# A long convolution with a rational feed-forward: the rounds of the first convolution in another order, and the products u on GpSimd

## The chip, the cores and the metric

One core of a Trainium2 chip. Its engines work side by side, each on its own queue in order: TensorE (PE, matmuls, with its weight loads shown as PEld), VectorE (DVE), ScalarE (ACT), GpSimd (POOL) and SyncE (SP, which here issues DMAs). They meet by semaphores. The metric is the device time of one execution in microseconds; before the change it is 2475.74 us, the median of 3 runs (2475.0 to 2476.28).

## What is computed

The reference filters u = x * v with a long filter by FFT, multiplies the result by x, and sends every token through a gated rational function between two matrices:

```python
# attention part, x and v: (2, 12480, 128), pos_emb: (12480, 64), w1: (64, 64), w2: (64, 128)
h_filt = (np.maximum(pos_emb @ w1, 0.0) @ w2) * np.exp(-0.01 * pos)[:, None]
u = x * v
L = 2 * S
y = np.fft.irfft(np.fft.rfft(u, n=L, axis=1) * np.fft.rfft(h_filt, n=L, axis=0)[None, :, :], n=L, axis=1)[:, :S, :]
x = (x * y).reshape(24960, 128)
# mixture part, w_in: (128, 2048), w_out: (2048, 128), a: 4 numbers, b: 2
h = x @ w_in
P = a[0] + a[1] * h + a[2] * h * h + a[3] * h * h * h
Q = 1.0 + np.abs(b[0]) * np.abs(h) + np.abs(b[1]) * h * h
out = (P / (Q + 1e-06)) @ w_out
```

## The kernel before

The convolution over 12480 positions is a transform in two factors, each done by matmuls with a constant matrix and a multiplication with twiddle factors between. The 128 channels are cut into 32 groups of 4 (CG = 4, NG = 32); eight groups are a quarter of the channels, 32 (UQ). A quarter of u lies in one buffer (tiles `hu0` to `hu3`, printed `hu_` with a number); it is filled by eight products of x and v, each of 16 positions of the second factor (UC) and all 32 channels (`mult_quarter`, L234), and a MEMSET on GpSimd (L229) clears its padding.

The program has four stages. **The filter's network** (0 to about 85 us of the trace): a loop of transposes and two matmuls makes the filter's values `hf`; `hf_w` multiplies the position embedding by the decaying window, the lower half in one TENSOR_TENSOR (L470), the mirrored half in four TENSOR_SCALAR (L474), for 16 blocks. Between them generators hand out one piece each time: the weights of the mixture, cut into two parts of high and low precision (`to_f32`, lines 320 to 336 and 445, where GpSimd's L331 feeds DVE's L336), and the eight products of the first quarter of u, on GpSimd. **The rounds** (85 to 375 us): the convolution of batch 0 together with the filter's transform. **The second part** (375 to 2440 us): a loop over steps of the mixture, with the convolution of batch 1 in its slots until about 1320 us. **The end** stores the last tiles.

A round g works on up to four groups, in a pipeline. In the order in which the instructions are written:

- s1h(g), the filter's first transform: matmuls L146 with `hf` into a PSUM tile `cs`, then six operations of DVE (`s1h_out`, L552, L553, L557 to L560) that write `zh`.
- s2h(g-1), the filter's second: L564 from `zh`; ACT copies the spectrum to `hg` (L600) and sends it to memory for batch 1 (L601).
- s1(g-1), the first transform of u: matmuls L146 with `hu`, two twiddle products on DVE (L164, L165) and two sums on GpSimd (L170, L171) that write `zu`.
- s2(g-2), the second of u: L181 to L184 from `zu`; DVE multiplies by `hg` (L196, L197), GpSimd sums (L199, L200) into `yy`.
- s3p(g-3), the inverse: L571 from `yy`; ACT copies twice (L578), GpSimd adds and subtracts (L582, L583) into `ys`, which two groups share. Every second round ACT copies a part of ys to `y0` (L621), which the second part begins with, and sends the whole to memory (L622).
- one product of the next quarter of u, on DVE (`mult_u`), as long as there are any (24, in rounds 0 to 23), else a piece of the weights; then the loads for a later product.

So there are 35 rounds, g = 0 to 34. The PSUM tiles `cs` of all five matmul groups come from one pool of four buffers, ys from a pool of one buffer, the other tiles named from pools of two. No scheduler moves anything: each engine runs its instructions in the order written.

In the second part a step s holds two halves of a block. ACT's work of a step is q0, v0 (squares and linear terms of the first half, L868, L877), q1, v1 of the second, ln of the step before (L905), sq (L901) and exp of the step before (L908). DVE finishes v (L887) and makes the ratio (L913, L918, L922). The change touches ACT's order in the loop at the end of `second_part`.

Of the kernel before, what the change touches and what calls it, by code (L numbers as in the profile page):

```python
# [9 lines left out]
F32 = mybir.dt.float32  # L10
F32R = mybir.dt.float32r
I32 = mybir.dt.int32
AF = mybir.ActivationFunctionType
# [87 lines left out]
def build(ctx: ExitStack, tc, x, v, pos_emb, w1, w2, w_in, w_out, moe_a, moe_b,  # L101
# [145 lines left out]
    with ExitStack() as st:  # L247
# [219 lines left out]
        def hf_w(p0):  # L467
# [4 lines left out]
            for i in range(NPL):  # L472
                n2 = H2 - 1 - p0 - i
                nc.vector.tensor_scalar(out=pw[:, i, 1], in0=t[0:MF, 2 * NPL - 1 - i], scalar1=win[0:MF, n2:n2 + 1],  # L474
                                        scalar2=None, op0=ALU.mult)
# [112 lines left out]
        for g in range(NG + 3):  # L588
            a = g
            if a < NG:  # L590
                zh[a] = ctile(sp, "zh", 2, CG)
                t = cvs()
                s1_mm(t, hf[a // gq], a % gq * CG, CG, MF)
                s1h_out(t, zh[a])
            a = g - 1
            if 0 <= a < NG:
                hgs[a] = ctile(sp, "hg", 2, CG)
# [4 lines left out]
                zu[a] = ctile(sp, "zu", 2, CG)  # L602
                t = cvs()
                s1_mm(t, us[a // gq], a % gq * CG, CG)
                s1_out(sp, t, zu[a], CG)
            a = g - 2
            if 0 <= a < NG:
                yy[a] = ctile(sp, "yy", 2, CG)
                t = cvs()
                s2_mm(t, zu.pop(a), CG)  # L610
                s2_prod(sp, t, hgs.pop(a), yy[a], CG)
            a = g - 3
            if 0 <= a < NG:
                if a % 2 == 0:
                    ysd[a // 2] = ystile(sp)
                t = cvs()
                s3p_mm(t, yy.pop(a))
                s3p_out(t, ysd[a // 2], a % 2 * CG, (nc.gpsimd, nc.gpsimd if a < NG - 3 else nc.vector))
                if a % 2 == 1:
                    t = ysd.pop(a // 2)  # L620
                    nc.scalar.activation(out=y0[:, a // 2], in_=t[:, :, 0:NPT, :], func=AF.Identity)  # L621
                    nc.scalar.dma_start(out=y_d[0][:, a // 2], in_=t)  # L622
            if uw and gq * (uw[0][0] - 1) <= g:
                mult_u(nc.vector)
# [10 lines left out]
    def second_part(short):  # L635
# [365 lines left out]
        for s in range(ns + 3):  # L1001
# [5 lines left out]
            run(s, dve_v, 0)  # L1007
            run(s, act_q, 1)
            run(s - 1, act_ln)
# [3 lines left out]
            run(s, act_v, 1)  # L1013
            run(s, act_sq)
            run(s + 1, mm1, 1)
            run(s, dve_v, 1)
            run(s - 1, act_exp)
            run(s - 2, dve_g)
# [35 lines left out]
```

## Time and profile before

| | |
|---|---|
| device time, median of 3 runs | 2475.74 us (2475.0 to 2476.28) |
| the profiled execution | 2475.52 us, its span 2473.6 us |
| busy in the span | PE 86%, DVE 94%, ACT 85%, POOL 22% |
| granted TensorE clock, mean | 0.969 of full speed |
| the filter's network, 0 to 84.7 us | DVE busy 69.4 us, PE 59.0, ACT 53.3, POOL 28.2 |
| rounds 0 to 22, 84.7 to 268.3 us | DVE 181.1 us of 183.6, PE 173.8, POOL 138.8 |
| rounds 23 to 27, 268.3 to 326 us | DVE 54.6 us of 57.7, PE 43.9 |
| the other rounds, 326 to 374.9 us | PE 43.1 us of 48.9, DVE 37.0 |
| 400 to 1300 us | DVE 848.6 us of 900, ACT 820.8, PE 808.7 |
| 1400 to 2440 us | ACT 1039.0 us of 1040, DVE 1023.6 |

The shares are averages over stages with different limits, so a stage is read by its own windows. A row of the timeline gives the start, the duration, the engine and line, the operation with its output and input, and in brackets how long the engine stood idle ahead of it and whom it waited for. Durations on one engine overlap a little, since the next instruction starts before the one before it has written all; the distance of starts is what an operation costs.

### The profile page before, as it was taken

The numbers are of one execution on the slowest core, as the hardware profiler recorded it, in microseconds if no ns is written. First come the engines' busy times: TensorE is split into PE (matmuls) and PEld (weight loads), VectorE is DVE, ScalarE is ACT, GpSimd is POOL, SyncE is SP. The second block draws the span as 40 slices with busy tenths as digits, with TensorE's granted clock in tenths as the row PEclk, the third lists the DMA queues.
The fourth block names the chain that finished last, engine by engine and source line by source line (L and its number), as shares of the span: only waits on it lengthen the run. The fifth ranks groups of instructions, "written<-read, shape, count | busy, mean of one in ns | idle before, by whom it ended". The sixth has DMA issues, their size and how long they took to land.

```text
span 2473.6 us, 33923 instructions
## 1 busy us (share of the span) xinstructions
PE 2129.4 (86%) x13344; PEld 1799.1 (73%) x13344; DVE 2335.8 (94%) x1945; ACT 2098.8 (85%) x1919; POOL 534.7 (22%) x522
## 2 busy tenths in 40 slices
PE   6899886999899979998999889788888888888786
PEld 4677765877777868777787777667777777767665
DVE  8999976999999988998999999999999999999997
ACT  5322227999999978998999999999999999999996
POOL 3488663121522242226122100000000000000000
PEclk9999997999999989999999999999999999999999
DMA  7466328112521252214222111111111111111000
GB/s 145 101 144 145 93 92 157 39 50 55 109 59 45 69 91 57 59 46 85 58 65 59 35 39 43 43 30 32 39 30 36 40 32 40 43 32 41 26 13 11
DMA packets 357824, 150.25 MB, mean 61 GB/s; under 512 B 292518, under 2 KB 339752, under 8 KB 354776
## 3 DMA queue, kind: packets, MB, share of 16 engines
q1 hardware_dynamic: 350632, 124.24, 23.8%
q10 hardware_dynamic: 7024, 23.76, 3.0%
q8 instruction: 107, 1.75, 0.3%
q14 instruction: 61, 0.50, 0.1%
HBM read 99.78 MB, written 48.17 MB: 60 GB/s over the span
## 4 chain that ended last, share of the span: by engine, by line
ACT 35%; DVE 27%; PE 24%; issue 9%; POOL 2%; DMA 1%; SPq 0%; ACTq 0%; DVEq 0%; POOLq 0%
ACT r L908 9%; ACT r L905 9%; ACT q L868 7%; PE acc L936 7%; DVE v L922 7%; ACT v L877 6%; DVE r L918 4%; DVE q L913 4%; PE cv L205 3%; ACT q L901 2%; PE cv L206 2%; DVE ta L192 2%; DVE v L887 2%; PE cs L571 2%; PE cv L146 1%
## 5 line engine op out<-in xcount | busy, mean ns | idle before, releaser
L936 PE MATMUL acc<-wout,v 128*128 128x128 f32 (+2 forms) x6656 | 829.2, 283 | 59.8 <-DVE v L922 35.2
L936 PEld LDWEIGHTS acc<-wout,v 128*128 128x128 f32 (+2 forms) x6656 | 785.0, 192 | 111.8 <-DVE v L922 53.9
L877 ACT ACTIVATE v<-h,sc 128x980 f32<-128x980 f32 (+1 forms) x416 | 639.0, 1536 | 6.6 <-PE acc L936 6.6
L868 ACT ACTIVATE q<-h 128x980 f32<-128x980 f32 (+1 forms) x416 | 581.5, 1455 | 6.6 <-PE h L860 6.6
L887 DVE SCALAR_TENSOR_TENSOR v<-v,sc,h 128x980 f32<-128x980 f32 (+1 forms) x416 | 505.8, 1216 | 62.1 <-ACT v L877 60.5
L901 ACT ACTIVATE q<-q,sc 128x1960 f32<-128x1960 f32 (+1 forms) x208 | 494.9, 2380 | 0.0
L905 ACT ACTIVATE r<-q,sc 128x1960 f32<-128x1960 f32 (+1 forms) x208 | 494.1, 2375 | 0.3 <-DVE v L922 0.3
L908 ACT ACTIVATE r<-r 128x1960 f32<-128x1960 f32 (+1 forms) x208 | 475.8, 2288 | 0.0
L913 DVE SCALAR_TENSOR_TENSOR q<-q,sc,r 128x1960 f32<-128x1960 f32 (+1 forms) x208 | 467.7, 2249 | 4.8 <-ACT r L908 1.1
L922 DVE SCALAR_TENSOR_TENSOR v<-v,sc,r 128x1960 f32<-128x1960 f32 (+1 forms) x208 | 465.6, 2238 | 0.1
L858 PE MATMUL h<-ahi,win_l 128*128 128x490 f32 (+1 forms) x832 | 364.3, 438 | 102.5 <-DVE v L887 100.1
L918 DVE SCALAR_TENSOR_TENSOR r<-q,r 128x1960 f32<-128x1960 f32 (+1 forms) x208 | 451.2, 2169 | 0.1
L859 PE MATMUL h<-alo,win_h 128*128 128x490 f32 (+1 forms) x832 | 320.7, 385 | 0.0
L860 PE MATMUL h<-ahi,win_h 128*128 128x490 f32 (+1 forms) x832 | 318.1, 382 | 0.0
L858 PEld LDWEIGHTS h<-ahi,win_l 128*128 128x128 f32 x832 | 158.5, 191 | 161.6 <-DVE v L887 133.9
L199 POOL TENSOR_TENSOR yy<-ta 128x180 f32<-128x180 f32 x64 | 119.8, 1871 | 369.5 <-DVE ta L192 369.5
L860 PEld LDWEIGHTS h<-ahi,win_h 128*128 128x128 f32 x832 | 158.8, 191 | 26.4
L859 PEld LDWEIGHTS h<-alo,win_h 128*128 128x128 f32 x832 | 159.2, 191 | 15.8 <-DVE alo L829 0.4
L804 PE MATMUL cv<-yc,gt 90*98 90x128 f32 x1004 | 131.8, 279 | 35.2 <-DVE an L810 32.6
L804 PEld LDWEIGHTS cv<-yc,gt 90*98 90x98 f32 x1004 | 115.7, 166 | 55.3 <-DVE an L810 51.5
L209 ACT ACTIVATE ys<-cv 90x512 f32<-90x512 f32 x64 | 77.0, 1203 | 71.6 <-PE cv L206 71.6
L205 PE MATMUL cv<-idft,yy 128*90 128x256 f32 x256 | 79.9, 394 | 61.2 <-DVE ta L192 36.4
(109 smaller groups left out, 2395.6 us busy)
## 6 DMA issues: line engine op xcount, KB each, us to landing
yc<-y_d SPq DMA_DIRECT2D x23, 900.0 KB
gt<-in_g_dram SPq DMA_DIRECT2D x48, 344.5 KB
h_d<-hg ACTq DMA_DIRECT2D x32, 360.0 KB
y_d<-ys ACTq DMA_DIRECT2D x16, 720.0 KB
hg<-h_d SPq DMA_DIRECT2D x64, 180.0 KB
y_d<-ys SPq DMA_DIRECT2D x16, 720.0 KB
xq<-in_x_dram SPq DMA_DIRECT2D x32, 196.0 KB
vq<-in_v_dram SPq DMA_DIRECT2D x32, 196.0 KB
```

What stands on the lines that cost most here:

```text
L858: nc.tensor.matmul(out=t[:, k, 0:w], lhsT=wl, rhs=hi[:, 0:w], start=True, stop=False)
L859: nc.tensor.matmul(out=t[:, k, 0:w], lhsT=wh, rhs=lo[:, 0:w], start=False, stop=False)
L868: nc.scalar.activation(out=halves(st_q[s], i, width(s)), in_=st_h[s, i], func=AF.Abs, **({} if short else {"scale": col("b0")}))
L877: nc.scalar.activation(out=v, in_=st_h[s, i], func=AF.Square, bias=col("s"))
L887: stt(out=v, in0=v, scalar=col("k"), in1=h, op0=ALU.add, op1=ALU.mult)
L901: nc.scalar.activation(out=whole(st_q, s), in_=whole(st_q, s), func=AF.Square, bias=col("dl"))
L905: nc.scalar.activation(out=whole(st_r, s), in_=whole(st_q, s), func=AF.Ln, **({"bias": col("ka")} if short else {}))
L908: nc.scalar.activation(out=whole(st_r, s), in_=whole(st_r, s), func=AF.Exp, scale=-1.0)
L913: nc.vector.scalar_tensor_tensor(out=q, in0=q, scalar=col("ka") if short else 0.0, in1=whole(st_r, s), op0=ALU.add, op1=ALU.mult)
L918: nc.vector.scalar_tensor_tensor(out=r, in0=whole(st_q, s), scalar=2.0, in1=r, op0=ALU.subtract, op1=ALU.mult)
L922: nc.vector.scalar_tensor_tensor(out=v, in0=v, scalar=col("p0" if short else "a0"), in1=whole(st_r, s), op0=ALU.add, op1=ALU.mult)
L936: nc.tensor.matmul(out=acc[j][0:k, q // 128, :], lhsT=g[:, i, q:q + k], rhs=wout[:, f, :], start=(f == 0 and q == 0), stop=(f == NF - 1), ...
```

## The change

Four edits. `hf_w` makes the mirrored half of the window product with one TENSOR_TENSOR of 82x256, by negative strides. The rounds are written as s1h(g), s1(g), s2(g-1), s3p(g-2), s2h(g), which makes 34 of them; the last ys tile lies in a buffer of the pool of hu, and of the last groups' sums on ys, one addition and two subtractions are DVE's (before, three subtractions). The products u in the rounds are GpSimd's. In the second part's step, ln stands ahead of q1, and exp ahead of sq. Lines behind L472 move by one, in the second part by nine.

```diff
--- before.py
+++ after.py
@@ -469,10 +469,11 @@
             pw = pos_t[p0] = sp.tile([MF, NPL, 2, FO], F32, tag="wb", name="pw", bufs=2)
             nc.vector.tensor_tensor(out=pw[:, :, 0], in0=t[0:MF, 0:NPL],
                                     in1=win[0:MF, H2 + p0:H2 + p0 + NPL].unsqueeze(2).to_broadcast([MF, NPL, FO]), op=ALU.mult)
-            for i in range(NPL):
-                n2 = H2 - 1 - p0 - i
-                nc.vector.tensor_scalar(out=pw[:, i, 1], in0=t[0:MF, 2 * NPL - 1 - i], scalar1=win[0:MF, n2:n2 + 1],
-                                        scalar2=None, op0=ALU.mult)
+
+            a, w = t[0:MF, 2 * NPL - 1], win[0:MF, H2 - 1 - p0:H2 - p0]
+            a = bass.AP(a.tensor, a.offset, [list(a.ap[0]), [-FO, NPL], [1, FO]])
+            w = bass.AP(w.tensor, w.offset, [list(w.ap[0]), [-1, NPL], [0, FO]])
+            nc.vector.tensor_tensor(out=pw[:, :, 1], in0=a, in1=w, op=ALU.mult)
 
         def hf_t(i):
             p0 = i * NP
@@ -585,43 +586,51 @@
         zh, zu, hgs, yy, ysd = {}, {}, {}, {}, {}
         gq = UQ // CG
 
-        for g in range(NG + 3):
+        def ys_tile(i):
+
+            if i < NG // 2 - 1:
+                return ystile(sp)
+            t = sp.tile([M, UQ, N2], F32, tag="hu", name="ysl", bufs=6)
+            return t.rearrange("p c t -> p (c t)")[0:K1, 0:2 * N2 * CY].rearrange("p (r t c) -> p r t c", r=2, t=N2)
+
+        for g in range(NG + 2):
             a = g
             if a < NG:
                 zh[a] = ctile(sp, "zh", 2, CG)
                 t = cvs()
                 s1_mm(t, hf[a // gq], a % gq * CG, CG, MF)
                 s1h_out(t, zh[a])
+                zu[a] = ctile(sp, "zu", 2, CG)
+                t = cvs()
+                s1_mm(t, us[a // gq], a % gq * CG, CG)
+                s1_out(sp, t, zu[a], CG)
             a = g - 1
             if 0 <= a < NG:
+                yy[a] = ctile(sp, "yy", 2, CG)
+                t = cvs()
+                s2_mm(t, zu.pop(a), CG)
+                s2_prod(sp, t, hgs.pop(a), yy[a], CG)
+            a = g - 2
+            if 0 <= a < NG:
+                if a % 2 == 0:
+                    ysd[a // 2] = ys_tile(a // 2)
+                t = cvs()
+                s3p_mm(t, yy.pop(a))
+                s3p_out(t, ysd[a // 2], a % 2 * CG, (nc.gpsimd if a < NG - 1 else nc.vector,
+                                                     nc.gpsimd if a < NG - 2 else nc.vector))
+                if a % 2 == 1:
+                    t = ysd.pop(a // 2)
+                    nc.scalar.activation(out=y0[:, a // 2], in_=t[:, :, 0:NPT, :], func=AF.Identity)
+                    nc.scalar.dma_start(out=y_d[0][:, a // 2], in_=t)
+            a = g
+            if a < NG:
                 hgs[a] = ctile(sp, "hg", 2, CG)
                 t = cvs()
                 s2h_mm(t, zh.pop(a))
                 nc.scalar.activation(out=hgs[a].rearrange("p r c k -> p r (c k)"), in_=spectrum(t, CG), func=AF.Identity)
                 nc.scalar.dma_start(out=h_d[:, a], in_=hgs[a])
-                zu[a] = ctile(sp, "zu", 2, CG)
-                t = cvs()
-                s1_mm(t, us[a // gq], a % gq * CG, CG)
-                s1_out(sp, t, zu[a], CG)
-            a = g - 2
-            if 0 <= a < NG:
-                yy[a] = ctile(sp, "yy", 2, CG)
-                t = cvs()
-                s2_mm(t, zu.pop(a), CG)
-                s2_prod(sp, t, hgs.pop(a), yy[a], CG)
-            a = g - 3
-            if 0 <= a < NG:
-                if a % 2 == 0:
-                    ysd[a // 2] = ystile(sp)
-                t = cvs()
-                s3p_mm(t, yy.pop(a))
-                s3p_out(t, ysd[a // 2], a % 2 * CG, (nc.gpsimd, nc.gpsimd if a < NG - 3 else nc.vector))
-                if a % 2 == 1:
-                    t = ysd.pop(a // 2)
-                    nc.scalar.activation(out=y0[:, a // 2], in_=t[:, :, 0:NPT, :], func=AF.Identity)
-                    nc.scalar.dma_start(out=y_d[0][:, a // 2], in_=t)
             if uw and gq * (uw[0][0] - 1) <= g:
-                mult_u(nc.vector)
+                mult_u(nc.gpsimd)
             else:
                 next(wg, None)
             load_u()
@@ -1005,16 +1014,16 @@
             run(s - 2, dve_e)
             slot(s, 0)
             run(s, dve_v, 0)
+            run(s - 1, act_ln)
             run(s, act_q, 1)
-            run(s - 1, act_ln)
+            run(s, act_v, 1)
             run(s - 3, mm2)
             run(s - 2, dve_n)
             slot(s, 1)
-            run(s, act_v, 1)
-            run(s, act_sq)
             run(s + 1, mm1, 1)
             run(s, dve_v, 1)
             run(s - 1, act_exp)
+            run(s, act_sq)
             run(s - 2, dve_g)
             slot(s, 2)
             if s >= 3 and steps[s - 3][1] == NC - 1:
```

PE, where group 16, the first of the third quarter, is transformed (groups 8 and 24 stand alike). In the names, hf1 and hf2 are the second and third quarter of the filter, hu1 and hu2 those of u; the other numbers only tell tiles apart. Before, round 16 with a part of round 17:

```order
L571 MATMUL cs_1919<-idfth_90,yy_1841 90x128 x8
L146 MATMUL cs_1940<-f1_66,hf2_93 128x180 x4
L564 MATMUL cs_1953<-zh_1875,dfth_89 128x360 x2
L146 MATMUL cs_1959<-f1_66,hu1_992 128x180 x4
L181 MATMUL cs_1971<-zu_1894,dft_68 128x360
L182 MATMUL cs_1971<-zu_1894,dft_68 128x360
L183 MATMUL cs_1971<-zu_1894,dft_68 128x360
L184 MATMUL cs_1971<-zu_1894,dft_68 128x360
L571 MATMUL cs_1982<-idfth_90,yy_1906 90x128 x8
L146 MATMUL cs_2007<-f1_66,hf2_93 128x180 x4
L564 MATMUL cs_2020<-zh_1939,dfth_89 128x360 x2
L146 MATMUL cs_2026<-f1_66,hu2_1473 128x180 x4
```

After, the end of round 15 and round 16:

```order
L572 MATMUL cs_1910<-idfth_90,yy_1834 90x128 x8
L565 MATMUL cs_1928<-zh_1873,dfth_89 128x360 x2
L146 MATMUL cs_1939<-f1_66,hf2_93 128x180 x4
L146 MATMUL cs_1952<-f1_66,hu2_1471 128x180 x4
L181 MATMUL cs_1964<-zu_1886,dft_68 128x360
L182 MATMUL cs_1964<-zu_1886,dft_68 128x360
L183 MATMUL cs_1964<-zu_1886,dft_68 128x360
L184 MATMUL cs_1964<-zu_1886,dft_68 128x360
L572 MATMUL cs_1976<-idfth_90,yy_1898 90x128 x8
```

Before, the first matmuls on hu2 stand a whole round behind the first on hf2; after, they stand right behind them, in the same round, and s2h (L565) stands last in the round instead of second.

GpSimd, the rounds of the same kind. Before, a round and the start of the next:

```order
L170 TENSOR_TENSOR zu<-ta,tb 128x360
L171 TENSOR_TENSOR zu<-ta,tb 128x360
L199 TENSOR_TENSOR yy<-pta,ptb 128x360
L200 TENSOR_TENSOR yy<-pta,ptb 128x360
L582 TENSOR_TENSOR ys<-qt 90x128x4
L583 TENSOR_TENSOR ys<-qt 90x2x64x4
L170 TENSOR_TENSOR zu<-ta,tb 128x360
```

After, round 7 with the last product of the second quarter at its end, and the start of round 8:

```order
L170 TENSOR_TENSOR zu_1360<-ta_1366,tb_1367 128x360
L171 TENSOR_TENSOR zu_1360<-ta_1366,tb_1367 128x360
L199 TENSOR_TENSOR yy_1372<-pta_1378,ptb_1379 128x360
L200 TENSOR_TENSOR yy_1372<-pta_1378,ptb_1379 128x360
L583 TENSOR_TENSOR ys_1320<-qt_1393,qt_1395 90x128x4
L584 TENSOR_TENSOR ys_1320<-qt_1393,qt_1395 90x2x64x4
L234 TENSOR_TENSOR hu1_962<-xq_1277,vq_1278 97x16x32
L170 TENSOR_TENSOR zu_1425<-ta_1431,tb_1432 128x360
L171 TENSOR_TENSOR zu_1425<-ta_1431,tb_1432 128x360
L199 TENSOR_TENSOR yy_1437<-pta_1443,ptb_1444 128x360
L200 TENSOR_TENSOR yy_1437<-pta_1443,ptb_1444 128x360
```

The last product into hu1 (L234) stands behind zu, yy and both sums of ys, and zu of round 8 stands behind it; before, no product stood on this engine here.

ACT in the loop of the second part, one step. Before, with L868 q, L877 v, L905 ln, L901 sq, L908 exp:

```order
L868 ACTIVATE q<-h 128x980
L877 ACTIVATE v<-h,sc 128x980
L868 ACTIVATE q<-h 128x980
L905 ACTIVATE r<-q,sc 128x1960
L877 ACTIVATE v<-h,sc 128x980
L901 ACTIVATE q<-q,sc 128x1960
L908 ACTIVATE r<-r 128x1960
```

After, with L877 q, L886 v, L914 ln, L910 sq, L917 exp:

```order
L877 ACTIVATE q<-h 128x980
L886 ACTIVATE v<-h,sc 128x980
L914 ACTIVATE r<-q,sc 128x1960
L877 ACTIVATE q<-h 128x980
L886 ACTIVATE v<-h,sc 128x980
L917 ACTIVATE r<-r 128x1960
L910 ACTIVATE q<-q,sc 128x1960
```

ln moved ahead of the second q, and exp ahead of sq; the other places are the same.

## Rows read from the trace of the kernel before

**Rows 1.** Windows: length; busy us of PE, PEld, DVE, ACT, POOL; granted clock; DMA.

```profile
120.00:152.00 32.00, 29.66 (x168) 23.96 (x168) 31.57 (x44) 7.93 (x14) 25.47 (x24) 1.00 0.61 143
333.80:341.60 7.80, 7.80 (x45) 6.43 (x44) 7.18 (x11) 2.12 (x4) 5.87 (x7) 1.00 0.38 109
290.00:300.00 10.00, 6.37 (x28) 6.05 (x29) 9.89 (x14) 1.57 (x4) 5.02 (x6) 0.66 0.41 116
```

**Rows 2.** Timeline of DVE, end of a product round: start us, us, operation.

```profile
177.26 1.10 DVE L234 TENSOR_TENSOR hu<-xq,vq 98x512 f32<-98x512 f32 x1
178.21 0.89 DVE L552 TENSOR_TENSOR tb<-cs,twh 128x720 f32<-128x720 f32 x1
```

**Rows 3.** Timeline of PE, late round without the product: inverse transform, next round's first.

```profile
338.36 1.91 PE L571 MATMUL cs<-idfth,yy 128*90 128x128 f32 x16
340.11 1.39 PE L146 MATMUL cs<-f,hf 82*128 82x180 f32 x8
```

**Rows 4.** Timeline of DVE and POOL in the same late round.

```profile
333.76 0.91 DVE L552 TENSOR_TENSOR tb<-cs,twh 128x720 f32<-128x720 f32 x1 [0.52 <-POOL zu L171]
337.15 0.54 DVE L560 TENSOR_TENSOR zh<-cs,tb 64x360 f32<-64x360 f32 x1
342.15 0.95 POOL L200 TENSOR_TENSOR yy<-pta,ptb 128x360 f32<-128x360 f32 x1
336.44 1.26 POOL L583 TENSOR_TENSOR ys<-qt 90x512 f32<-90x512 f32 x1
```

**Rows 5.** Timeline of PE: a short wait, and a long one later.

```profile
272.39 1.95 PE L571 MATMUL cs<-idfth,yy 128*90 128x128 f32 x16 [0.48 <-DVE zh L560]
293.63 3.69 PE L571 MATMUL cs<-idfth,yy 128*90 128x128 f32 x16 [5.38 <-DVE zh L560]
297.12 1.94 PE L146 MATMUL cs<-f,hf 82*128 82x180 f32 x8
```

**Rows 6.** Timeline of the first stage: POOL's product of u, DVE's window product twice.

```profile
17.26 1.28 POOL L234 TENSOR_TENSOR hu<-xq,vq 98x512 f32<-98x512 f32 x1 [3.48 <-DMA vq<-in_v_dram]
17.39 1.42 DVE L470 TENSOR_TENSOR pw<-pos,ta 82x256 f32<-82x256 f32 x1 [2.44 <-DMA pos<-in_pos_emb_dram]
54.27 0.42 DVE L470 TENSOR_TENSOR pw<-pos,ta 82x256 f32<-82x256 f32 x1
```

**Rows 7.** Timeline of DVE: L552 of rounds 23 and 25.

```profile
268.33 0.90 DVE L552 TENSOR_TENSOR tb<-cs,twh 128x720 f32<-128x720 f32 x1
289.57 0.90 DVE L552 TENSOR_TENSOR tb<-cs,twh 128x720 f32<-128x720 f32 x1
```

**Rows 8.** Timeline of the start: L552 of rounds 0 and 2, PE between.

```profile
84.68 0.90 DVE L552 TENSOR_TENSOR tb<-cs,twh 128x720 f32<-128x720 f32 x1
96.21 0.90 DVE L552 TENSOR_TENSOR tb<-cs,twh 128x720 f32<-128x720 f32 x1
87.61 2.74 PE L564 MATMUL cs<-zh,dfth 128*128 128x360 f32 x4 [3.78 <-issue]
```

**Rows 9.** Timeline of the end: L552 of rounds 28 and 31, last ys.

```profile
325.94 0.91 DVE L552 TENSOR_TENSOR tb<-cs,twh 128x720 f32<-128x720 f32 x1 [2.37 <-POOL yy L200]
349.41 0.91 DVE L552 TENSOR_TENSOR tb<-cs,twh 128x720 f32<-128x720 f32 x1 [0.52 <-POOL zu L171]
371.41 3.43 POOL L582 TENSOR_TENSOR ys<-qt 90x512 f32<-90x512 f32 x2 [2.64 <-DMA y_d<-ys]
374.88 0.27 ACT L621 ACTIVATE y<-ys 90x80 f32<-90x80 f32 x1 [3.18 <-POOL ys L582]
```

**Rows 10.** Timeline of DVE in the first stage: iterations with the filter's product, without.

```profile
58.47 0.41 DVE L470 TENSOR_TENSOR pw<-pos,ta 82x256 f32<-82x256 f32 x1
81.20 0.43 DVE L329 SCALAR_TENSOR_TENSOR f<-i,i 128x256 f32<-128x256 int32 x1
84.33 0.43 DVE L329 SCALAR_TENSOR_TENSOR f<-i,i 128x256 f32<-128x256 int32 x1
```

**Rows 11.** Waits, 400 to 1300 us: line <- releaser: us, times, longest.

```profile
DVE v L887 <- ACT v L877: 36.6, 55, 1.2
```

## The prediction

> **What bounds the kernel now.** I read the table of windows first. Over four of the early rounds VectorE (DVE) is busy 31.57 of 32.00 us and TensorE (PE) 29.66; in one late round, which makes no product u, PE is busy 7.80 of 7.80 and DVE 7.18 [rows 1]. So the rounds have two limits close together. With the product, a round lasts as long as DVE's work: the product L234 is the last of a round, 0.95 us from its start to the next L552, and the eleven rounds from that L552 to the one at 268.33 take 8.19 us each [rows 2, 7]. Without the product three rounds take 23.47 us (325.94 to 349.41 [rows 9]), 7.82 each, which is PE's own work. GpSimd (POOL) comes behind DVE: in such a round it ends yy 9.34 us after L552 began (343.10 - 333.76) [rows 4]; it has slack, but its chain reaches into the next round. The profiled execution took 2475.52 us, 0.2 below the median of the runs; the sum is made against 2475.5.
>
> **The product on GpSimd, steady rounds.** 24 products leave DVE: 24 x 0.95 = 22.8 us of DVE work. That is not the gain, since the next limit, PE, is at 7.82: at best 8.19 - 7.82 = 0.37 a round. Nor is that reached. The new order on PE is s1h(g), s1(g), s2(g-1), s3p(g-2), s2h(g); there are four PSUM buffers for five users, and in every second (even) round the buffer of s3p(g-2) is that of s1h(g), free only after the filter's last sum on DVE, L560 (L561 in the changed code). PE would reach s3p about 4.9 us after the round's start (its 7.82 less s3p's 1.75, from 338.36 to 340.11 [rows 3], and less s2h's 1.2); DVE can begin L552 when s1h is done (about 1.4), and needs 3.93 to the end of L560 (337.69 - 333.76 [rows 4]) and a hand-over: some 5.6. PE stands 0.7. The trace of before has such a wait, 0.48 us at L571 for L560 [rows 5]. So odd rounds take 7.82 and even ones 8.52, 8.17 on average: as before. For the 22 rounds in question I take 0, with -8 (no stand at all, 22 x 0.37) and +5 (another 0.2 a round) as bounds. GpSimd's product costs 1.28 us (its own product in the first stage [rows 6]), so POOL's round goes from 6.6 to some 7.2 us: it fits. The Trainium skill (GPSIMD Engine Reference, 4.1 Engine selection) calls GpSimd about twice as slow as VectorE for two-input elementwise work. The row says 1.28 against 0.95; by the page it would be 1.9, and the sum 2 us more.
>
> **The product on GpSimd, where a quarter of u begins.** This is the largest term. Eight products fill one buffer of 32 channels, and the first u transform of the quarter reads all eight. Before, s1(8) stood in round 9, a round behind the last product. Now it stands in round 8, right behind s1h(8), and the last product is the last thing that GpSimd does in round 7, behind zu, yy and both ys. Counted from L552 of round 7: yy ends at 9.34; the two ys add 1.26 each, to 11.86 [rows 4], and the product 1.28 [rows 6], to 13.1. PE comes to s1(8) at about 7.7. It waits 5.4 us, and behind that wait stand all its other matmuls; DVE can do only the filter's six operations meanwhile. Such a gap also costs clock: after 5.38 us of idle time L571 took 3.69 us and the next L146 1.94, where they take 1.91 and 1.39, 2.3 us lost [rows 3, 5]. The granted clock of that stretch was 0.66 where it is 1.00 in a full one [rows 1]. The 0.7 of an even round is hidden in the gap. So 5.4 + 2.3 - 0.7 = 7.0 each, for rounds 8 and 16: +14.0, between +9.4 (no clock loss) and +16. At round 24 the rounds are stretched by weight steps on DVE already (two rounds take 21.24 us, 268.33 to 289.57 [rows 7]), and part of the gap lies beside them. The first of the two becomes 13.1 + 1.0 to its next L552 at the half clock, and the second stays at some 12.7, a weight step and a round's work on DVE: 26.8, so +5.6, bounds +2 and +8.
>
> **Fewer rounds: the start.** Before, PE has s1h(0) and s1h(1) done before DVE begins, and idles 3.78 us to s2h(0) at 87.61, which ran at half clock (2.74) [rows 8]. DVE had L552 of round 2 at 96.21, 11.53 us after that of round 0 at 84.68. Now s1h(1) stands behind s2h(0), which waits for L560(0) at 88.6: s2h(0) 2.5 and s1h(1) 2.4, both at the half clock, and L552(1) comes 7.96 after L552(0); then a round of DVE's eight operations, 7.24: 15.2. **+3.7**, between +1 (full clock) and +5. One round fewer does not give this back, since all 32 groups must still go through.
>
> **Rounds 27 to 31 and the end.** L552 of round 28 waits 2.37 us for GpSimd's yy, one round behind the weight step [rows 9]; in the new order that wait is some 0.8: -1.6. Rounds 28 to 31 took 23.47 us and, with two even stands, will take 24.9: +1.4. From L552(31) to the last y0 copy it was 25.47 (374.88 - 349.41). Of that GpSimd waited 2.64 us for the DMA that empties the single ys buffer [rows 9]; the last ys tile now has a buffer of its own, and this wait goes. What is late next is ACT: hg(31) stands behind the y0 copy that waits for ys, and PE idles 5.7 us before its last s3p and runs it at the half clock: 23.5, so **-2.0**, between -5 (full clock, nothing late) and 0.
>
> **One product of the window instead of four small ones.** 64 TENSOR_SCALAR become 16 TENSOR_TENSOR of 82x256 like L470, which took 0.42 at 54.27. But the same L470 took 1.42 us at 17.39, beside a GpSimd product that began at 17.26 [rows 6]. The Trainium skill (SBUF — State Buffer, Who interferes with whom) says that a VectorE operation with two inputs in SBUF and a GpSimd one that reads SBUF shut each other out, and the row agrees. In the weight iterations DVE waits for GpSimd's L331 and L445 afterwards in any case: an iteration with the filter's products takes 4.20 us (54.27 to 58.47), one without 3.13 (81.20 to 84.33) [rows 6, 10]. Were the new product never shut out, the 11 such iterations could save all of 1.07 each, 11.8; shut out behind L331 they save some 0.2 each: **-2**, with 0 and -11.8 as bounds.
>
> **ACT's order in the main loop.** q1 and ln change places, and sq and exp. The wait that it could touch is DVE's L887 for v1 of ACT, 36.6 us in 55 times while the convolution of batch 1 runs beside [rows 11]. v1 still stands behind q0, v0, q1 and ln, the same sum, and the ys copy is ahead of them both times. Later, from 1400 us, ACT and DVE are both full. I take 0, bounds -5 and +5.
>
> **Sum.** 0 + 14.0 + 5.6 + 3.7 - 1.6 + 1.4 - 2.0 - 2.0 + 0 = +19.1, and 2475.5 + 19.1 = 2494.6 us. The second part begins when y0 is there, and its DVE is nearly full, so what comes later stays late.
>
> **Rivals.** (A) Faster: the swap on ACT frees DVE. Its place is the 55 waits of L887; exp comes 1.8 us earlier, so what DVE makes of it can start earlier and fill them. All of it would be 19.1 - 36.6 = -17.5, 2458 us; it decides from 19.1 / 55 = 0.35 us a step on. Against it: L887 waits where v1 is late, and v1's place in ACT's sum is the same. (B) No change: the quarters don't stall, because the products run ahead in POOL's slack. Then 14.0 + 5.6 fall away: -0.5, 2475 us. Against it: GpSimd's queue is in order, and the order shows the last product behind both ys. If the window product is also never shut out, it is 2465. (C) Worse: ACT's hg of odd rounds stands behind a y0 copy that waits for GpSimd's ys, and s2h of the next round waits for hg's buffer. I have it just in time; a GpSimd that is 1 us later costs about 0.9 in each of 14 pairs, +12.6: 2507 us.
>
> **How the numbers follow.** The forecast, slower by 10 to 28 us, has a chance of 0.64; (A) 0.09; (B) 0.17, of which 0.05 is faster by over 0.2%; (C) 0.10. 0.2% is about what a measurement of this kernel can tell from no change, 5 us. So faster 0.14, same 0.12, slower 0.74. The range reaches from (B) to just short of (C), 2474 to 2505 us; the forecast's own range is 2485 to 2503.
>
> **What would show it.** In the profile after: PE idle for about 5 us ahead of the first L146 on hu in rounds 8, 16 and 24, put down to POOL's L234, with half-speed matmuls behind it; L234 on POOL near 1.3 us; L572 waiting some 0.7 us for L561 in every second round; L552 8.1 to 8.2 us apart in the pair's mean; the window product (L476) longer than 0.42 beside L331; the last ys without a DMA wait. The prediction is wrong if L552 stays 7.82 apart in all rounds, if no wait for L234 shows, or if the waits of L887 for ACT shrink by more than 10 us.

## The result: 0.66% slower, and the profile after

The changed kernel took 2491.85 us, median of 4 runs (2488.61 to 2493.47), against 2475.68 us for the kernel before in the same comparison; the ratio is 1.0066, with a 95% interval of 1.0053 to 1.0078. The prediction was 2494.6 us, slower by 19. The profiled execution after took 2490.94 us, its span 2489.0; the span of before was 2473.6, so 15.4 us are to be accounted for. The starts of the filter's first operation on DVE (L552 before, L553 after) and the last y0 copy cut both spans at the same points of the program:

| from, to | before, us | after, us | difference | forecast |
|---|---|---|---|---|
| start to L552 of round 0 (first stage) | 84.68 | 81.97 | -2.7 | -2.0 |
| round 0 to 2 | 11.53 | 14.65 | +3.1 | +3.7 |
| the round from 8 to 9, from 16 to 17, from 24 to 25 | 29.39 | 50.50 | +21.1 | +19.6 |
| the other rounds from 2 to 24 | 163.97 | 162.09 | -1.9 | 0 |
| 25 to 27 | 26.29 | 26.42 | +0.1 | 0 |
| 27 to 28 | 10.08 | 8.43 | -1.6 | -1.6 |
| 28 to 31 | 23.47 | 25.96 | +2.5 | +1.4 |
| L552 of round 31 to the last y0 copy | 25.47 | 23.01 | -2.5 | -2.0 |
| last y0 copy to the end of the span | 2098.72 | 2095.97 | -2.8 | 0 |
| sum | 2473.60 | 2489.00 | +15.4 | +19.1 |

The largest row is the one at the quarters. These are the waits of PE between 80 and 400 us of the kernel after (line, releaser: us in total, times, the longest):

```profile
PE cs L146 <- POOL hu L234: 15.9, 3, 5.3
PE cs L565 <- DVE zh L561: 7.4, 3, 3.4
PE cs L572 <- POOL yy L199: 5.0, 1, 5.0
```

Three waits of 5.3 us each for GpSimd's product. The timeline of PE around the first of them, round 8 (start us, us, what ran, in brackets the idle time before it and its releaser):

```profile
149.99 2.77 PE L146 MATMUL cs<-f,hu 98*128 98x180 f32 x8 [5.30 <-POOL hu L234]
152.55 1.40 PE L181 MATMUL cs<-zu,dft 128*128 128x360 f32 x2
...
156.81 1.91 PE L572 MATMUL cs<-idfth,yy 128*90 128x128 f32 x16
```

GpSimd in the same place, from yy of round 7 on:

```profile
145.31 0.94 POOL L200 TENSOR_TENSOR yy<-pta,ptb 128x360 f32<-128x360 f32 x1
146.22 1.26 POOL L583 TENSOR_TENSOR ys<-qt 90x512 f32<-90x512 f32 x1
147.44 1.26 POOL L584 TENSOR_TENSOR ys<-qt 90x512 f32<-90x512 f32 x1
148.66 1.27 POOL L234 TENSOR_TENSOR hu<-xq,vq 97x512 f32<-97x512 f32 x1
154.66 0.82 POOL L170 TENSOR_TENSOR zu<-ta,tb 128x360 f32<-128x360 f32 x1 [4.72 <-DVE tb L165]
```

The product ends at 149.93, 12.97 us after L553 of round 7 at 136.96 (13.1 was forecast), and PE starts on hu in the next 0.1 us. L146 takes 2.77 us and L181 1.40, where they take 1.39 and 0.77 in a full stretch. The windows after the three waits show the granted clock behind PEld, DVE, ACT and POOL (columns as in [rows 1]):

```profile
150.00:156.00 6.00, 6.00 (x14) 4.55 (x15) 1.72 (x2) 0.00 (x0) 1.34 (x2) 0.50 0.95 218
223.00:229.00 6.00, 5.58 (x15) 4.42 (x16) 1.72 (x2) 0.41 (x1) 1.27 (x3) 0.59 0.98 237
296.00:302.00 6.00, 6.00 (x21) 4.83 (x22) 1.95 (x3) 0.00 (x0) 1.34 (x2) 0.70 0.49 153
```

0.50 is the lower of the two levels (the half clock) throughout, 0.59 and 0.70 for a part of the stretch. Elsewhere the rounds alternate. PE in rounds 11 and 12:

```profile
181.02 1.91 PE L572 MATMUL cs<-idfth,yy 128*90 128x128 f32 x16
...
189.53 1.95 PE L572 MATMUL cs<-idfth,yy 128*90 128x128 f32 x16 [0.52 <-POOL ys L584]
```

From L572 to L572 it is 8.51 us into the even round and 7.83 into the odd one; this wait of PE ahead of L572 in every second round is called the even stand below. Here it is put down to POOL's L584, but DVE's L561 ended in the same hundredth, 189.38; of the nine waits of this kind in the trace three name L561. Of [rows 2] what is left is the distance of the L553s, 7.83 and 8.55 in turn, 8.19 in the mean, as before: 23 us of work have left DVE, and the steady round is no shorter.

The start, as the counterpart of [rows 8], DVE and PE:

```profile
84.90 2.74 PE L565 MATMUL cs<-zh,dfth 128*128 128x360 f32 x4 [4.04 <-issue]
87.43 1.66 PE L146 MATMUL cs<-f,hf 82*128 82x180 f32 x8
89.13 0.91 DVE L553 TENSOR_TENSOR tb<-cs,twh 128x720 f32<-128x720 f32 x1 [1.48 <-PE cs L146]
```

DVE waits for s1h(1), which stands behind s2h(0), as forecast; the half clock lasted less long (1.66 for the L146, not 2.4). That is not so in every run: in the four others that have this order with s2h last, the same L146 took 2.61 us, and rounds 0 to 2 took 15.49 to 16.46 us, 4.0 to 4.9 more than before. The end, as the counterpart of [rows 9]:

```profile
387.21 3.29 PE L572 MATMUL cs<-idfth,yy 128*90 128x128 f32 x14 [0.17 <-POOL yy L200]
391.65 0.69 DVE L583 TENSOR_TENSOR ysl<-qt 90x512 f32<-90x512 f32 x1 [6.20 <-ACT qt L579]
393.03 0.27 ACT L623 ACTIVATE y<-ysl 90x80 f32<-90x80 f32 x1 [1.42 <-DVE ysl L584]
```

The last ys no longer waits for a DMA; PE stood 5.0 us ahead of it for yy, whose products on DVE had waited 5.8 us for hg(31) behind the y0 copy, as forecast, and ran it at the half clock, so that half of the bound of -5 was had.

### The profile page after: what moved, and what is told of

Its sections match the earlier page's. It is cut to its first block, busy times and chain, and to the rows that moved or that the text cites. A ratio compares the mean times of both kernels' runs of the same rounds, so it can differ in the third digit from the quotient of the medians.

```text
span 2489.0 us, 33881 instructions
## 1 busy us (share of the span) xinstructions
PE 2137.2 (86%) x13344; PEld 1803.8 (72%) x13344; DVE 2301.1 (92%) x1873; ACT 2093.5 (84%) x1919; POOL 561.1 (23%) x546
## 4 chain that ended last, share of the span: by engine, by line
ACT 34%; DVE 28%; PE 21%; issue 9%; POOL 5%; DMA 1%; SPq 1%; ACTq 0%; DVEq 0%; POOLq 0%
ACT r L914 10%; ACT q L910 9%; DVE v L931 8%; PE acc L945 7%; ACT v L886 6%; ACT q L877 5%; DVE r L927 4%; DVE q L922 4%; PE cv L205 3%; DVE v L896 2%; PE cv L206 2%; ACT r L917 2%; DVE ta L192 2%; PE cv L146 1%; PE h L867 1%
## 5 line engine op out<-in xcount | busy, mean ns | idle before, releaser
L886 ACT ACTIVATE v<-h,sc 128x980 f32<-128x980 f32 (+1 forms) x416 | 606.8, 1459 | 6.5 <-PE acc L945 6.5
L877 ACT ACTIVATE q<-h 128x980 f32<-128x980 f32 (+1 forms) x416 | 565.3, 1359 | 3.2 <-PE h L869 3.2
L910 ACT ACTIVATE q<-q,sc 128x1960 f32<-128x1960 f32 (+1 forms) x208 | 478.1, 2299 | 0.0
L914 ACT ACTIVATE r<-q,sc 128x1960 f32<-128x1960 f32 (+1 forms) x208 | 473.6, 2277 | 0.8 <-DVE v L931 0.8
L917 ACT ACTIVATE r<-r 128x1960 f32<-128x1960 f32 (+1 forms) x208 | 458.9, 2206 | 0.0
L868 PE MATMUL h<-alo,win_h 128*128 128x490 f32 (+1 forms) x832 | 320.6, 385 | 0.0
L199 POOL TENSOR_TENSOR yy<-ta 128x180 f32<-128x180 f32 x64 | 117.8, 1840 | 364.3 <-DVE ta L192 364.3
L868 PEld LDWEIGHTS h<-alo,win_h 128*128 128x128 f32 x832 | 159.5, 192 | 16.0 <-DVE alo L838 0.4
L579 ACT ACTIVATE qt<-cs 90x512 f32<-90x512 f32 x64 | 34.5, 589 | 133.3 <-PE cs L572 132.9
L209 ACT ACTIVATE ys<-cv 90x512 f32<-90x512 f32 x64 | 77.0, 1202 | 72.5 <-PE cv L206 72.5
```

Of the source, the lines that this page charges most:

```text
L868: nc.tensor.matmul(out=t[:, k, 0:w], lhsT=wh, rhs=lo[:, 0:w], start=False, stop=False)
L877: nc.scalar.activation(out=halves(st_q[s], i, width(s)), in_=st_h[s, i], func=AF.Abs, **({} if short else {"scale": col("b0")}))
L886: nc.scalar.activation(out=v, in_=st_h[s, i], func=AF.Square, bias=col("s"))
L910: nc.scalar.activation(out=whole(st_q, s), in_=whole(st_q, s), func=AF.Square, bias=col("dl"))
L914: nc.scalar.activation(out=whole(st_r, s), in_=whole(st_q, s), func=AF.Ln, **({"bias": col("ka")} if short else {}))
L917: nc.scalar.activation(out=whole(st_r, s), in_=whole(st_r, s), func=AF.Exp, scale=-1.0)
```

## The experiments

Each is compared with the kernel before on the same chip, 2474.2 to 2475.1 us. Distances of rounds are those of L552 or L553.

**The products back on VectorE.**

```diff
-                mult_u(nc.gpsimd)
+                mult_u(nc.vector)
```

> The changed kernel with the products u back on VectorE, all else as changed. Theory (the loss sits at the starts of quarters, where s1 waits for GpSimd's last product): the three long rounds, which took 16.5, 15.6 and 18.4 us, fall to about 8.2, 8.2 and 13.1, some 21 us less, and the other rounds stay near 8.2, now by VectorE's sum: 2471 us (2467 to 2476). Rival (the new order of the rounds itself costs, whoever makes the products): 2485 us or more, with the long rounds still there.

2475.58 us (2474.03 to 2476.66), 16.3 less than the changed kernel. The three rounds at the quarters took 8.53, 8.54 and 13.06. The rest was not at 8.2 but at 8.16 and 8.54 in turn, so the run came out 4.6 above the 2471: the even stand comes on top of DVE's 8.16 where it lay beside DVE's slack in the changed kernel. PE's waits between 80 and 400 us, with ten for L561:

```profile
PE cs L572 <- DVE zh L561: 8.0, 10, 0.9
PE cs L146 <- DVE hu L234: 2.2, 3, 0.7
```

One of them, and ACT's copy to y0, which waits for L584 of the same round:

```profile
184.39 1.95 PE L572 MATMUL cs<-idfth,yy 128*90 128x128 f32 x16 [0.85 <-DVE zh L561]
184.57 0.27 ACT L623 ACTIVATE y<-ys 90x80 f32<-90x80 f32 x1 [5.99 <-POOL ys L584]
```

L561 ended at 184.25 and L584 at 184.53, so L572 starts ahead of L584's end. The even stand is a wait for L561 and not for L584.

**The product at the top of the round, still on GpSimd.**

```diff
         for g in range(NG + 2):
+            made = uw and gq * (uw[0][0] - 1) <= g
+            if made:
+                mult_u(nc.gpsimd)
             a = g
...
-            if uw and gq * (uw[0][0] - 1) <= g:
-                mult_u(nc.gpsimd)
-            else:
+            if not made:
                 next(wg, None)
```

> The changed kernel with each product of u issued at the top of its round instead of the end, still on GpSimd: a quarter's last product is done a round's work of GpSimd earlier. Theory: PE no longer waits for L234, the long rounds fall to 8.2, 8.2 and 13.1: about 21 us less than the changed kernel, 2471 us (2467 to 2476). Rival (GpSimd's load or its meeting VectorE at SBUF costs): stays above 2480 us.

2470.16 us (2469.39 to 2471.98), 0.9982 of before (0.9972 to 0.9991), 21.7 less than the changed kernel. The three rounds took 8.75, 8.74 and 13.06 and no wait of L146 for L234 is left. GpSimd has the same work; only its place in the queue differs. This is the cause of the slowdown, shown twice with two different remedies.

**The product in the middle of the round.**

```diff
+            made = uw and gq * (uw[0][0] - 1) <= g
+            if made:
+                mult_u(nc.gpsimd)
             a = g - 2
             if 0 <= a < NG:
...
-            if uw and gq * (uw[0][0] - 1) <= g:
-                mult_u(nc.gpsimd)
-            else:
+            if not made:
                 next(wg, None)
```

> The changed kernel with the product issued ahead of the two sums of ys, in the middle of GpSimd's round: a quarter's last product is done 2.5 us earlier, so PE's wait for it is 2.8 us instead of 5.3. It splits the price of a long round into wait and clock. If the matmuls behind the shorter wait run at the half clock too: 3 x 2.5 = 7.5 us less than the changed kernel, 2484 us. If they keep the full clock: another 3 x 2.2 less, 2478 us.

2487.07 us (2485.17 to 2487.78). Neither sum holds, for two reasons. First, the wait is half as long at all three starts of a quarter, but only at the first of them does the clock stay full. PE there, then the window around it:

```profile
150.29 1.49 PE L146 MATMUL cs<-f,hu 98*128 98x180 f32 x8 [2.85 <-POOL hu L234]
151.62 0.77 PE L181 MATMUL cs<-zu,dft 128*128 128x360 f32 x2
```

```profile
148.00:156.00 8.00, 5.71 (x33) 4.75 (x34) 6.79 (x10) 1.05 (x3) 6.30 (x7) 1.00 0.62 137
```

That round took 10.95 us instead of 16.47: 2.45 us of wait and 3.1 of clock are gone. Behind the same 2.85 us at the second and third start PE ran at the half clock:

```profile
220.43 2.77 PE L146 MATMUL cs<-f,hu 98*128 98x180 f32 x8 [2.85 <-POOL hu L234]
292.20 2.77 PE L146 MATMUL cs<-f,hu 98*128 98x180 f32 x8 [2.85 <-POOL hu L234]
```

From there to the next L572 (225.82 and 299.24) it took 5.39 and 7.04 us for what takes 3.64 in a full stretch, 1.8 and 3.4 lost; in the changed kernel the clock cost 2.3 and 1.9 there. So the second and third long round fell only by 3.0 and 0.9. Second, ys now comes 1.3 us later in every round, and the odd rounds' hg stands behind the y0 copy that waits for ys. PE in an even round of this kernel:

```profile
170.38 1.95 PE L572 MATMUL cs<-idfth,yy 128*90 128x128 f32 x16 [0.52 <-DVE zh L561]
172.80 1.48 PE L565 MATMUL cs<-zh,dfth 128*128 128x360 f32 x4 [0.47 <-ACT hg L633]
```

Six rounds of 9.30 take the place of 8.55 (PE waits for hg six times, 2.9 us), 4.5 us given back. This is the mechanism of rival (C) of the prediction: with GpSimd one product (1.28 us) later it costs 0.75 us in each of six rounds, where (C) had 0.9 in each of 14 for 1 us. In the changed kernel hg was just in time.

**The product alone, in the old order.**

```diff
-                mult_u(nc.vector)
+                mult_u(nc.gpsimd)
```

> The kernel before with only the products u moved to GpSimd, in the old order of the rounds. Theory: there s1 of a quarter's first group stands a round later, so the product is done in time, no long rounds; VectorE's relief counts down to TensorE's 7.82 us a round: 22 x 0.37 = 8 us less, 2467.6 us (2465 to 2471). Rival 1 (the products on GpSimd make the rounds wait wherever they stand): 2485 us or more. Rival 2 (VectorE's relief is worth nothing, as another wait takes its place): 2475 us.

2465.59 us (2464.28 to 2466.67), ratio 0.9963 (0.9949 to 0.9977). From round 2 to 24 the rounds take 170.8 us instead of 180.3; the longest are two of 8.75. GpSimd's product costs what the first stage showed, and yy is no longer held up by a VectorE product with two SBUF inputs (L199 is down from 1.58 us, the mean before, to 0.95):

```profile
L234 POOL TENSOR_TENSOR hu<-xq,vq 98x512 f32<-98x512 f32 (+1 forms) x24 | 30.8, 1285 | 0.2
L199 POOL TENSOR_TENSOR yy<-pta,ptb 128x360 f32<-128x360 f32 x23 | 21.9, 954 | 0.6
```

So moving the product is a gain of 9 us by itself. It turns into a loss only together with the new order, which takes away the round of slack behind the last product.

**The order alone.** The changed kernel with the other three edits undone (the four window products are back too, and exp stands behind sq again, not shown).

```diff
-                mult_u(nc.gpsimd)
+                mult_u(nc.vector)
...
-            run(s - 1, act_ln)
             run(s, act_q, 1)
-            run(s, act_v, 1)
+            run(s - 1, act_ln)
```

> The kernel before with only the new order of the rounds and its end, products on VectorE, four window products, ACT's old order. Theory: start +3 to +3.7, two late even stands +1.4, round 28 -1.6, end -2, and the even stand comes on top of VectorE's 8.16 (the run with the products on VectorE shows pairs of 8.16 and 8.54, 16.70 against 16.33): 11 x 0.37 = +4: 2480.5 us (2478 to 2483). Rival (one round fewer gains): 2472 us or less.

2481.81 us (2478.6 to 2483.55), ratio 1.0027 (1.0016 to 1.0039): by itself the new order costs 7 us.

**Three edits in the old order.** The kernel before with the product on GpSimd, the one window product and ACT's new order. The lines of the window product and of sq and exp are not shown.

```diff
-                mult_u(nc.vector)
+                mult_u(nc.gpsimd)
...
-            run(s, act_q, 1)
             run(s - 1, act_ln)
+            run(s, act_q, 1)
+            run(s, act_v, 1)
```

> The kernel before with three of the four edits: products u on GpSimd, one window product, ACT's order in the second part; the rounds in the old order. Theory: 2467.6 of the product alone, less 2.7 for the first stage (the changed kernel's first L553 came 2.7 us earlier) and less up to 2.7 for ACT's order: 2462 us (2459 to 2468). Rival (the small edits are worth nothing behind the rounds): the same as the product alone, 2467.6 us.

2456.99 us (2454.83 to 2464.1), ratio 0.9932 (0.9914 to 0.9951). 8.6 less than the product alone, more than the 5.4 expected and below the expected range. In the two traces the first stage is 1.9 us shorter and the second part 5.2.

**The new order with s2h in its old second place**, on top of the product at the top of the round.

```diff
+            a = g - 1
+            if 0 <= a < NG:
+                hgs[a] = ctile(sp, "hg", 2, CG)
...
-            a = g
-            if a < NG:
-                hgs[a] = ctile(sp, "hg", 2, CG)
...
```

> The kernel with the product at the top of the round, and s2h back in the second place, a round behind s1h (s1h(g), s2h(g-1), s1(g), s2(g-1), s3p(g-2)). Theory (with s2h last, the PSUM buffer that s3p wants is held by s1h's tile in every second round, 0.72 us each): the pairs of 7.83 and 8.55 become 7.82 each, some 11 such pairs in the product rounds and two behind, -9 us against that kernel's 2470: 2461 us. It also takes s2h(0) out of the way of s1h(1) at the start, up to -3 more. Rival (the stand in every second round has another cause): the rounds stay 8.2 in the mean, 2468 us or more.

2457.21 us (2455.62 to 2459.65), 13 less than with s2h last. PE goes through odd and even rounds alike without a stand, 7.82 us from s3p to s3p:

```profile
170.44 1.91 PE L572 MATMUL cs<-idfth,yy 128*90 128x128 f32 x16
...
178.26 1.91 PE L572 MATMUL cs<-idfth,yy 128*90 128x128 f32 x16
...
186.09 1.91 PE L572 MATMUL cs<-idfth,yy 128*90 128x128 f32 x16
```

So the stand in every second round belongs to s2h's last place. That it is the PSUM buffer is read from the program: L561 reads `cs` of s1h and writes `zh`, which L572 does not use, so the pool of `cs` is all that the two share. No view shows the buffers themselves. This run also shows that 34 rounds with the u chain one round shorter are no loss in themselves.

**The last ys tile in a buffer of its own**, on top of the three edits in the old order. Not shown are `ys_tile` and the shares of GpSimd and VectorE, both as in the changed kernel.

```diff
-                    ysd[a // 2] = ystile(sp)
+                    ysd[a // 2] = ys_tile(a // 2)
```

> The three edits in the old order of the rounds, as in the run of all but the order (2457.0 us), and from the fourth edit only its end: the last ys tile in a buffer of its own, with the changed shares of GpSimd and VectorE on it. Theory: GpSimd's wait of 2.64 us for the DMA goes, and with it up to 2.6 us at the start of the second part: 2454.5 us. Rival (ACT or TensorE is late there next): 2457 us, no change.

2457.8 us (2452.75 to 2459.47) beside 2456.99: no difference that these runs can tell. From L552 of round 31 to the last y0 copy it was 25.4 us against 25.9 in the run of the three edits; the DMA's wait is gone; next PE waits 1.4 us for yy there, ACT 3.5 for GpSimd's ys and 3.7 for PE.

**The window product alone.**

```diff
-            for i in range(NPL):
-                n2 = H2 - 1 - p0 - i
-                nc.vector.tensor_scalar(out=pw[:, i, 1], in0=t[0:MF, 2 * NPL - 1 - i], scalar1=win[0:MF, n2:n2 + 1],
-                                        scalar2=None, op0=ALU.mult)
+            a, w = t[0:MF, 2 * NPL - 1], win[0:MF, H2 - 1 - p0:H2 - p0]
...
+            nc.vector.tensor_tensor(out=pw[:, :, 1], in0=a, in1=w, op=ALU.mult)
```

> The kernel before with only the window product as one TENSOR_TENSOR. Theory: it is shut out by GpSimd's operations, the first L552 comes some 2 to 2.7 us earlier, and 2472.5 to 2473 us follow. Rival 1: never shut out, 11.8 us less, 2463 us. Rival 2: what is won there is lost again later, 2475 us.

2471.28 us (2468.75 to 2473.77), ratio 0.9988 (0.9979 to 0.9997): 2.9 less. The first stage of the changed kernel shows where a part of the rest went:

```profile
56.97 0.84 POOL L331 TENSOR_TENSOR f<-f,i 128x256 f32<-128x256 f32 x1 [3.06 <-DVE f L329]
57.14 0.94 DVE L476 TENSOR_TENSOR pw<-pos,ta 82x256 f32<-82x256 f32 x1
57.77 2.60 POOL L445 TENSOR_TENSOR win_l<-f,win_h 128x256 fp32r<-128x256 f32 x1
```

L476 takes 0.94 us beside L331, and then GpSimd's L445 takes 2.60. It begins within L476 and goes on for 2.3 us behind it; what holds it there no run shows. In the groups of that stage L476 is 10.9 us busy, where the four small products were 24.5, and L445 has gone from 0.78 us each to 1.73:

```profile
L445 POOL TENSOR_TENSOR win_l<-f,win_h 128x256 fp32r<-128x256 f32 x8 | 13.9, 1733 | 0.0
L476 DVE TENSOR_TENSOR pw<-pos,ta 82x256 f32<-82x256 f32 x16 | 10.9, 679 | 0.1
```

13.6 us of DVE's work went, and 2.9 us of time. In the run with this one edit L445 took 1.91 us each, and DVE waited for it, which it never did in the first stage before:

```profile
DVE f L329 <- POOL win_l L445: 3.1, 5, 0.6
```

These 3.1 us are a part of what was lost again; the other part is not accounted for here.

**ACT's order alone.**

```diff
-            run(s, act_q, 1)
             run(s - 1, act_ln)
+            run(s, act_q, 1)
+            run(s, act_v, 1)
...
-            run(s, act_v, 1)
-            run(s, act_sq)
...
             run(s - 1, act_exp)
+            run(s, act_sq)
```

> The kernel before with only ACT's order in the second part changed. Theory of the prediction: it does nothing, 2475 us (within 2 us). Rival, from all edits but the order being 8.6 us faster than the product alone, of which the window product can hardly hold more than 3: it is worth about 6 us, 2469 us, and the waits of VectorE or TensorE in the second part are shorter by that.

2470.91 us (2468.87 to 2474.98), ratio 0.9985 (0.9976 to 0.9994): 3.3 less, where the prediction had 0. The waits of DVE for v shrank, as the counterpart of [rows 11] in this run shows:

```profile
DVE v L887 <- ACT v L877: 31.3, 55, 1.1
```

5.3 us less in 55 waits. Three operations of a step of this run's ACT:

```profile
844.30 1.87 ACT L905 ACTIVATE r<-q,sc 128x1960 f32<-128x1960 f32 x1
846.07 0.97 ACT L868 ACTIVATE q<-h 128x980 f32<-128x980 f32 x1
846.94 1.07 ACT L877 ACTIVATE v<-h,sc 128x980 f32<-128x980 f32 x1
```

and of the kernel before:

```profile
847.52 1.05 ACT L868 ACTIVATE q<-h 128x980 f32<-128x980 f32 x1
848.48 1.91 ACT L905 ACTIVATE r<-q,sc 128x1960 f32<-128x1960 f32 x1
850.29 1.05 ACT L877 ACTIVATE v<-h,sc 128x980 f32<-128x980 f32 x1
```

From the first of the three to the start of v it was 2.77 us (847.52 to 850.29), and now is 2.64 (844.30 to 846.94). The three operations are the same. In both kernels ACT's copy of ys (L209) stands directly ahead of them here, and the difference is found only in such steps, 56 between 400 and 1300 us in either trace: there the medians are 0.94 and 1.82 us before (q to ln, ln to v), 1.78 and 0.87 in this run (ln to q, q to v). From the first start to v that is 0.1 us less a step, some 6 us in all, an estimate; 5.3 are seen in the waits. In the other steps, and after 1400 us, both orders come to 2.69. Why a q directly behind the copy costs 0.07 more is open. The swap of sq and exp was not run by itself.

The traces of the other runs agree: from the last y0 copy to the end of the span it is 2092.5 to 2096.5 us in the eight with this order of ACT, 2098.1 to 2100.4 in the four with the old one.

**v1 ahead of ln.** The kernel before with one place of ACT's order changed.

```diff
             run(s, act_q, 1)
+            run(s, act_v, 1)
             run(s - 1, act_ln)
...
-            run(s, act_v, 1)
             run(s, act_sq)
```

> The kernel before with only one place of ACT's order in the second part changed: v1 ahead of ln, so q0, v0, q1, v1, ln, sq, exp. The prediction gave ACT's order nothing because v1 stood behind the same four operations; it measured 3.3 us, and VectorE's waits for v1 of the second half shrank from 34.7 to 30.6 us in 47 steps. Theory (those waits are the chain ys, q1, ln, v1 and then L887, and they set the step's length while the convolution runs beside): with ln's 1.8 us out of that chain nearly all 34.7 us go: 2444 us (2438 to 2452). Rival (another wait, for exp or for TensorE's h, is late next): 2470 us or more.

2455.08 us (2453.1 to 2455.74), ratio 0.9921 (0.9905 to 0.9938). From the last y0 copy to the end it takes 2077.7 us instead of 2098.7. That is above the theory's range and far below the rival's. Between 400 and 1300 us DVE's waits for v are out of the list of the six longest, and the longest for ACT's exp is:

```profile
DVE q L913 <- ACT r L908: 6.1, 14, 0.8
```

So the waits did set the step's length while the convolution of batch 1 runs beside, and 20 of the 35 us are gained.

**All of it together.** The run with the last ys tile, with v1 ahead of ln.

```diff
-            run(s - 1, act_ln)
             run(s, act_q, 1)
             run(s, act_v, 1)
+            run(s - 1, act_ln)
```

> The run of all edits but the order with the last ys tile (2457.8 us), with v1 ahead of ln on ACT. Theory: the waits of 30.6 us for the second half's v1 go here as well: 2430 us (2425 to 2440). Rival (another wait is late next): 2455 us or more.

2454.26 us (2453.47 to 2455.01), ratio 0.9918 (0.9902 to 0.9935): the lowest of all here, but 24 above the 2430, and no different from the run before it. The second part takes 2091.3 us. In this order exp stands directly behind ln, on whose result it works. ACT after 1400 us, where it is full:

```profile
1801.77 1.95 ACT L913 ACTIVATE r<-q,sc 128x1960 f32<-128x1960 f32 x1
1803.75 1.84 ACT L916 ACTIVATE r<-r 128x1960 f32<-128x1960 f32 x1
```

and in the run with v1 ahead of ln alone, where sq stands between them:

```profile
1800.43 2.68 ACT L905 ACTIVATE r<-q,sc 128x1960 f32<-128x1960 f32 x1
1802.25 2.68 ACT L901 ACTIVATE q<-q,sc 128x1960 f32<-128x1960 f32 x1
1804.07 2.58 ACT L908 ACTIVATE r<-r 128x1960 f32<-128x1960 f32 x1
```

1.98 us from ln to the next start against 1.82: 0.16 us in a step, in a stage in which ACT sets the time. The starts of ln, one in each step, show both halves. The first 80 steps took 853.8 us against 870.6 in the run with the last ys tile, so 16.8 us of the waits went here too; the steps behind them took 1194.1 against 1180.2, and 14 us are given back (between 1400 and 2400 us a step is 9.33 us long against 9.16). The three edits with v1 ahead of ln and sq ahead of exp weren't run; by these numbers they would give about 2457 - 17, 2440 us, an estimate.

## Why the prediction was right, point by point

- **The start of a quarter** was the cause, and it was sized nearly right: 21.1 us against 19.6. The wait of 5.30 us (5.4 forecast) and the half clock behind it stood in the profile as described. The first gap cost more clock than the 2.3 us taken from [rows 5]: from 149.99 to 156.81 PE did what takes 3.64 us in a full stretch (s1 and s2, 1.22 + 2.42), 3.2 lost; at the second, 223.42 to 229.38, it lost 2.3, and at the third, 295.99 to 301.50, 1.9. The last quarter came out as forecast only in its sum (+5.4 against +5.6): the round from 24 to 25 alone grew, to 18.43 us, while the one from 23 to 24 took 7.83, not 14.1. Two kernels that make the product earlier, on VectorE or at the top of GpSimd's round, are 16.3 and 21.7 us faster than the changed kernel.
- **The steady rounds** are no shorter, as forecast: 7.83 and 8.55 in turn, against 7.82 and 8.52. The step is supported by the run with s2h second, where the even stand is gone, and by the run with the products on VectorE, where L561 and L584 end apart and L572 waits for L561.
- **The start, the rounds 27 to 31 and the end** came out at +3.1, +0.8 and -2.5 against +3.7, -0.2 and -2.0. At the start the sum 7.96 doesn't follow from the 88.6 beside it: 88.6 + 2.5 + 2.4 is 8.8 behind 84.68. The row of [rows 8] has s2h(0) begin at 87.61, ahead of L560's end, and from there 7.96 follows; in the four runs in which the half clock lasted, the first round took 8.00 to 8.11. That it took 7.16 in this trace goes with the half clock that ended earlier. L553 of round 28 waited 0.74 us, as forecast, but that of round 29 then waited for yy, for which the forecast had nothing:

```profile
353.64 0.91 DVE L553 TENSOR_TENSOR tb<-cs,twh 128x720 f32<-128x720 f32 x1 [2.27 <-POOL yy L200]
```

- **The window product** gave 2.7 in the trace and 2.9 alone, 2 forecast. The row of [rows 6] was the right one to price it by: two inputs in SBUF beside GpSimd. What the prediction left out is that GpSimd's operation behind it gets longer as well, L445. Its reading that DVE waits for L331 and L445 in any case is half wrong: before, DVE waited 2.5 us for L331 in the first stage and not at all for L445.
- **ACT's order** was mis-sized: 0 forecast, -2.8 in the trace and -3.3 alone. The step that failed is "v1 still stands behind q0, v0, q1 and ln, the same sum": the sum of the same operations is not the same in another sequence, by 0.1 us in each step that has a copy of ys ahead. Rival (A) named the right wait, L887, but its price needs v1 in another place; there 20 of the 36.6 us are to be had.
- Rival (B) is what the product at the top of the round does: 2470 us, where (B) said 2475. Rival (C)'s mechanism is seen with the product in the middle of the round, at 0.75 us in each of six rounds.

The forecast was 2.7 us too high, about the size of ACT's order. The misses of the other terms, up to 1.9 us each, nearly cancel; that they do is luck.

## What to carry to other kernels

When a step is moved to an earlier round or to another queue, look for what was done just before the point at which it is now needed: a slack of one round that no wait shows in the profile can carry the next wait. Edits need not add: alone the four gave -9.4 (product), +6.8 (order), -2.9 and -3.3 us, -9 in all, and together +16. And where a chain of several operations on one engine ends in a wait, their order inside the chain is worth a trial before any operation is made faster.

## What the runs showed of the hardware

- On ACT the distance of two starts depends on the neighbours: directly behind the copy of ys, q to ln and ln to v take 0.94 and 1.82 us, ln to q and q to v 1.78 and 0.87; without the copy ahead q to ln takes 0.87. An exp that works on the result of the ln directly ahead of it starts 0.16 us later than sq does in its place.
- Behind three gaps of 5.30 us PE ran s1 and s2 at the half clock for a part of the time and lost 3.2, 2.3 and 1.9 us. Behind three gaps of 2.85 us at the same places it lost 0.1, 1.8 and 3.4. In the kernel after, at a weight step, 2.03 us of idle time were followed by the lower level too (L565 2.74 us at 313.27). So the length of the gap alone doesn't tell.
- A VectorE operation with two inputs in SBUF and a GpSimd operation beside it can both get longer: 0.94 us for L476 instead of 0.41, and 2.60 for the L445 that begins within it, 0.73 in the median before. GpSimd's L199 took 1.58 us in the mean with VectorE's product L234 beside it, and 0.95 with that product gone.
